# One scaling instruction for rows 0 to 3, the second tile's statistics in free order, tile 3's statistics on ScalarE, and a newly searched order

## The chip, the cores and the metric

The kernel runs on one core of one Trainium2 chip. The metric is the device time of one execution in microseconds (us); several executions are timed and their median is given. Engines are named as in the profile: PE (TensorE matmul), PEld (its weight loads), DVE (VectorE), ACT (ScalarE), POOL (GpSimd), SP (SyncE, which here only starts DMAs).

## The reference

The input x has 2048 rows of 640 bf16 values. It is normalized row by row, and then two branches and x itself are added.

```python
xn = _layernorm(x, axis=-1)            # (x - mean) / sqrt(var + 1e-5)
# branch A: spectral filter over rows and columns
X = rfft2(xn.astype(float32)); X = X * (w_r + 1j * w_i); a = irfft2(X).astype(bfloat16)
# branch B: gated linear unit without an activation
g = xn @ w_gate; u = xn @ w_up; b = (g * u) @ w_down      # 640 -> 1536 -> 640
out = x + a + b
```

## The kernel before

The 2048 rows are held as 16 tiles of 128 rows (128 partitions, 640 values each). Everything is one program of some 980 tasks. A task is a name, an engine, a function that emits its instructions, the buffers that it reads and writes, and, for a PE task, the PSUM bank (of eight) that it fills and the task that empties it.

The order is not decided while the program is built. The tuple `_PLAN` lists every task by number with its engine (0 PE, 1 ACT, 2 DVE, 3 POOL, 4 SP) and its PSUM bank. `replay` walks through it, gives every engine its queue in that order, and `compute_waits` puts a semaphore wait ahead of a task for each input, each output buffer and each PSUM bank that is not yet known to be free. Each task carries a duration in ns; in this file it only serves `replay`'s own clock, by which `compute_waits` sorts tasks when it leaves out waits that another wait already covers. The plan itself was found by a search that used such durations. [...]

The tasks that this study speaks of, in the order of the data:

- `ld_x0` to `ld_x5` (L728) load x: tiles 0, 1, 2 and 3 each alone, then four tiles, then eight. `ld_gw*` load gate and up weights.
- `warm_zero` (L696) clears a small tile on DVE; `warm` (L720) is 40 matmuls of that tile, which nobody reads; `fill` (L709) is 10 smaller ones. They keep PE occupied ahead of the first tile.
- Statistics of a tile b: on DVE `bn_b_0`, `bn_b_1` (written bn0_0 and so on, L756, one half of the columns each) and `ag` (L765); or on ACT `sm` (L738, the mean through an accumulator) and `sq` (L747, the sum of squares). Before, tiles 0 to 5 use DVE and tiles 6 to 15 use ACT. `sd` (L774, L775) is the square root on ACT and `rs` (L782) the reciprocal on DVE.
- Scaling: for tiles 0 to 3 `sub` (L792) subtracts the mean and `mul` (L798) multiplies; for tiles 4 to 15 one `mul` (L799) does both.
- Transposing: tiles 0 to 3 on PE (`T0_b`, L818) with copies out of PSUM by ACT and DVE (`eT0_b`), later tiles by DMA (`xt`).
- Branch B: `GU_f_b` multiplies weights of column block f with the rows that start at tile b (L968 for 128 or 256 rows, L948 for 512); `eG_u_0` and `eG_u_1` copy the two results of unit u from PSUM to a ring of three slots, and `H_u` (L984, L985) multiplies them on DVE. So a GU of unit u waits for H of unit u - 3. `ACC_a_h_k` (L1224) are the products with w_down, in pieces, and `FINA`, `FIN` and `st_out` finish and store.
- Branch A: `S1` to `S5` (DVE, five groups of tiles, L860 to L895), `R` (PE, L908) and `eR` (copy), then for t = 0 to 15 `D_t_w` (PE, L1025), `eD_t_w` (two copies of 64x321), `C_t` (L1045), `WM_t` (six DVE instructions from PSUM, L1062 and L1068), `NS_t` (three POOL instructions, L1077 to L1079), and for odd t `SM_t` (L1089, L1090), `JA_t` and `JB_t` (ACT or DVE). `IA_q` (L1116, L1118) with its copy `eIA_q`; when all of these are there, `I_a` (L1147), its copy `eI_a`, `V1` to `V5` (DVE), and `IV_a_h` (L1236), which adds the result to the bank that ACC fills.

Copies that either engine may do go through one helper: on ACT they are recorded at L684, on DVE at L685.

The lines that tie the second to the fourth tile to the tile ahead, and those that choose the statistics' engine:

```python
aset = set(opts.get("act_set", ())) | set(range(opts.get("act_stats", 6), 16))
...
if 1 <= b <= 3:
    bns[0].deps.add(muls[b - 1])
```

The first half of the statistics of tiles 1, 2 and 3 thus waits for the scaling of the tile ahead.

Of the kernel before, what the change touches and what calls it, by code (L numbers as in the profile page):

```python
# [399 lines left out]
def _d_act(n):  # L400
# [4 lines left out]
    (12, 4, -1), (0, 1, -1), (13, 4, -1), (176, 1, -1), (175, 4, -1), (8, 2, -1), (19, 2, -1), (9, 3, -1), (177, 4, -1),  # L405
    (18, 2, -1), (20, 2, -1), (11, 0, 0), (23, 2, -1), (21, 1, -1), (22, 2, -1), (24, 2, -1), (29, 2, -1), (25, 0, 2),
    (28, 2, -1), (26, 1, -1), (27, 2, -1), (178, 4, -1), (10, 0, 4), (14, 4, -1), (30, 2, -1), (33, 2, -1), (31, 1, -1),
    (32, 2, -1), (187, 0, 5), (34, 2, -1), (185, 0, 4), (188, 1, -1), (35, 0, 6), (15, 4, -1), (37, 2, -1), (192, 0, 5),
    (190, 0, 0), (186, 1, -1), (189, 2, -1), (38, 2, -1), (179, 4, -1), (36, 1, -1), (39, 2, -1), (180, 4, -1), (181, 4, -1),
    (197, 0, 1), (40, 2, -1), (48, 2, -1), (41, 1, -1), (43, 2, -1), (42, 2, -1), (193, 1, -1), (195, 0, 2), (44, 2, -1),  # L410
    (47, 2, -1), (202, 0, 3), (200, 0, 4), (182, 4, -1), (191, 1, -1), (196, 1, -1), (198, 1, -1), (49, 2, -1), (50, 1, -1),
    (16, 4, -1), (194, 2, -1), (201, 1, -1), (45, 0, 2), (52, 2, -1), (51, 2, -1), (183, 4, -1), (53, 2, -1), (207, 0, 6),
    (46, 1, -1), (184, 4, -1), (199, 2, -1), (118, 2, -1), (54, 0, 7), (205, 0, 2), (1, 4, -1), (203, 1, -1), (204, 2, -1),
    (55, 1, -1), (210, 0, 3), (212, 0, 7), (217, 0, 5), (208, 1, -1), (17, 4, -1), (215, 0, 4), (119, 2, -1), (206, 1, -1),
    (209, 2, -1), (120, 2, -1), (56, 2, -1), (211, 1, -1), (60, 2, -1), (59, 2, -1), (2, 4, -1), (3, 4, -1), (57, 2, -1),
    (68, 1, -1), (69, 1, -1), (213, 1, -1), (220, 0, 0), (121, 2, -1), (4, 4, -1), (58, 2, -1), (70, 1, -1), (216, 1, -1),
    (61, 2, -1), (218, 1, -1), (62, 1, -1), (122, 2, -1), (63, 2, -1), (222, 0, 1), (5, 4, -1), (214, 2, -1), (64, 2, -1),
    (125, 0, 2), (221, 1, -1), (71, 1, -1), (223, 1, -1), (123, 0, 6), (126, 1, -1), (219, 2, -1), (227, 0, 4), (127, 2, -1),
    (232, 0, 5), (225, 0, 0), (72, 1, -1), (230, 0, 1), (224, 2, -1), (128, 2, -1), (6, 4, -1), (7, 4, -1), (228, 1, -1),
    (66, 2, -1), (78, 1, -1), (79, 1, -1), (237, 0, 4), (226, 1, -1), (129, 2, -1), (235, 0, 0), (73, 2, -1), (80, 1, -1),  # L420
    (233, 1, -1), (229, 2, -1), (81, 1, -1), (130, 2, -1), (231, 1, -1), (82, 1, -1), (240, 0, 5), (76, 2, -1), (131, 2, -1),
    (238, 1, -1), (134, 0, 2), (74, 2, -1), (236, 1, -1), (83, 2, -1), (234, 2, -1), (242, 0, 4), (84, 2, -1), (65, 4, -1),
    (245, 0, 1), (67, 4, -1), (241, 1, -1), (75, 4, -1), (88, 1, -1), (77, 4, -1), (239, 2, -1), (135, 1, -1), (252, 0, 0),
    (247, 0, 5), (136, 2, -1), (243, 1, -1), (89, 1, -1), (244, 2, -1), (246, 1, -1), (132, 0, 2), (137, 2, -1), (90, 1, -1),
    (91, 1, -1), (86, 2, -1), (248, 1, -1), (250, 0, 1), (249, 2, -1), (255, 0, 4), (92, 1, -1), (98, 1, -1), (251, 1, -1),
    (85, 4, -1), (87, 4, -1), (437, 4, -1), (438, 4, -1), (93, 2, -1), (99, 1, -1), (138, 2, -1), (439, 4, -1), (253, 1, -1),
    (257, 0, 5), (256, 1, -1), (100, 1, -1), (258, 1, -1), (96, 2, -1), (254, 2, -1), (101, 1, -1), (139, 2, -1), (260, 0, 1),
    (262, 0, 0), (267, 0, 4), (94, 2, -1), (263, 1, -1), (133, 1, -1), (102, 1, -1), (261, 1, -1), (259, 2, -1), (140, 2, -1),
    (265, 0, 5), (103, 2, -1), (266, 1, -1), (440, 4, -1), (268, 1, -1), (270, 0, 0), (143, 0, 2), (264, 2, -1), (441, 4, -1),
    (104, 2, -1), (272, 0, 1), (124, 1, -1), (141, 0, 4), (269, 2, -1), (442, 4, -1), (108, 1, -1), (271, 1, -1), (273, 1, -1),  # L430
    (277, 0, 6), (149, 2, -1), (274, 2, -1), (109, 1, -1), (275, 0, 7), (280, 0, 0), (443, 4, -1), (142, 1, -1), (282, 0, 1),
    (444, 4, -1), (276, 1, -1), (278, 1, -1), (147, 0, 4), (281, 1, -1), (445, 4, -1), (145, 0, 6), (150, 2, -1), (446, 4, -1),
    (285, 0, 0), (106, 2, -1), (110, 1, -1), (283, 1, -1), (447, 4, -1), (146, 1, -1), (111, 1, -1), (287, 0, 1), (279, 2, -1),
    (112, 1, -1), (144, 1, -1), (292, 0, 6), (151, 2, -1), (286, 1, -1), (290, 0, 7), (293, 1, -1), (113, 2, -1), (448, 4, -1),
    (284, 2, -1), (152, 2, -1), (288, 1, -1), (116, 2, -1), (291, 1, -1), (297, 0, 2), (474, 4, -1), (475, 4, -1), (289, 2, -1),
    (476, 4, -1), (295, 0, 3), (114, 2, -1), (153, 2, -1), (302, 0, 0), (294, 2, -1), (162, 2, -1), (298, 1, -1), (296, 1, -1),
    (95, 4, -1), (97, 4, -1), (105, 4, -1), (299, 2, -1), (303, 1, -1), (154, 0, 6), (148, 1, -1), (107, 4, -1), (300, 0, 1),
    (477, 4, -1), (301, 1, -1), (156, 0, 2), (158, 0, 4), (159, 1, -1), (305, 0, 0), (155, 1, -1), (478, 4, -1), (160, 0, 4),
    (310, 0, 1), (479, 4, -1), (163, 2, -1), (480, 4, -1), (481, 4, -1), (307, 0, 6), (308, 1, -1), (304, 2, -1), (115, 4, -1),
    (312, 0, 7), (306, 1, -1), (164, 2, -1), (315, 0, 6), (317, 0, 0), (309, 2, -1), (313, 1, -1), (157, 1, -1), (311, 1, -1),  # L440
    (165, 2, -1), (316, 1, -1), (320, 0, 1), (318, 1, -1), (166, 2, -1), (322, 0, 0), (173, 0, 2), (314, 2, -1), (161, 1, -1),
    (167, 0, 6), (323, 2, -1), (321, 1, -1), (169, 0, 4), (174, 2, -1), (168, 1, -1), (325, 0, 1), (171, 0, 6), (170, 1, -1),
    (172, 1, -1), (327, 0, 0), (326, 2, -1), (451, 0, 1), (319, 2, -1), (324, 2, -1), (456, 0, 2), (328, 1, -1), (117, 4, -1),
    (449, 0, 3), (452, 2, -1), (458, 0, 4), (330, 0, 5), (435, 4, -1), (482, 0, 6), (450, 1, -1), (457, 1, -1), (436, 4, -1),
    (459, 2, -1), (705, 4, -1), (507, 4, -1), (508, 4, -1), (453, 0, 0), (509, 4, -1), (337, 0, 7), (510, 4, -1), (329, 2, -1),
    (460, 0, 2), (491, 0, 4), (511, 4, -1), (483, 1, -1), (512, 4, -1), (332, 0, 6), (331, 1, -1), (492, 1, -1), (515, 0, 5),
    (338, 1, -1), (454, 2, -1), (333, 1, -1), (516, 1, -1), (461, 2, -1), (335, 0, 0), (484, 0, 1), (455, 3, -1), (513, 4, -1),
    (340, 0, 4), (514, 4, -1), (485, 1, -1), (463, 2, -1), (342, 0, 5), (486, 0, 6), (522, 0, 1), (334, 2, -1), (336, 1, -1),
    (465, 2, -1), (540, 4, -1), (464, 1, -1), (489, 0, 0), (347, 0, 2), (541, 4, -1), (466, 0, 3), (462, 3, -1), (343, 1, -1),
    (487, 2, -1), (490, 1, -1), (468, 0, 5), (517, 0, 0), (493, 0, 6), (467, 1, -1), (523, 1, -1), (339, 2, -1), (345, 0, 3),  # L450
    (494, 2, -1), (496, 2, -1), (488, 3, -1), (542, 4, -1), (543, 4, -1), (352, 0, 1), (544, 4, -1), (545, 4, -1), (518, 1, -1),
    (346, 1, -1), (546, 4, -1), (341, 1, -1), (470, 0, 0), (472, 0, 3), (547, 4, -1), (344, 2, -1), (573, 4, -1), (469, 1, -1),
    (350, 0, 6), (473, 1, -1), (497, 2, -1), (524, 0, 7), (548, 0, 3), (348, 1, -1), (519, 0, 4), (353, 1, -1), (351, 1, -1),
    (495, 3, -1), (525, 1, -1), (357, 0, 2), (498, 2, -1), (520, 2, -1), (505, 0, 1), (574, 4, -1), (355, 0, 6), (358, 1, -1),
    (471, 1, -1), (499, 0, 7), (501, 0, 2), (349, 2, -1), (500, 2, -1), (550, 0, 0), (506, 1, -1), (356, 1, -1), (503, 0, 1),
    (526, 0, 4), (360, 0, 6), (521, 3, -1), (354, 2, -1), (583, 0, 7), (575, 4, -1), (549, 1, -1), (551, 1, -1), (576, 4, -1),
    (577, 4, -1), (362, 0, 3), (527, 2, -1), (578, 4, -1), (529, 2, -1), (530, 2, -1), (361, 1, -1), (555, 0, 0), (367, 0, 6),
    (579, 4, -1), (502, 1, -1), (365, 0, 2), (580, 4, -1), (359, 2, -1), (552, 0, 4), (363, 1, -1), (364, 2, -1), (528, 3, -1),
# [64 lines left out]
def _build(nc, A_x, A_w_r, A_w_i, B_w_gate, B_w_up, B_w_down, out, opts=None):  # L523
    opts = opts or {}
    tabs = _build_tables()
    es = contextlib.ExitStack()
    with es:
# [33 lines left out]
        b_sm = alloc("SM", 384)  # L561
        b_gbf = alloc("GBF", 6 * 512)
        b_stat = alloc("STAT", 608)
        b_dum = alloc("DUM", 256)
        b_jk = alloc("JK", 640)

        o_3 = cur[0]
# [780 lines left out]
```

## Time and profile before

| what | value |
|---|---|
| time, median of 3 | 199.64 us (199.36 to 199.67) |
| the profiled execution | 199.54 us, span of the program's instructions 197.2 us |
| granted PE clock | full over the span by the page's row |
| ACT ACTIVATE PSUM to SBUF, 128x512 f32 to bf16 | 87 of them, mean 599 ns |
| ACT copies of 64x321 (eD) | 60 of them, mean 434 ns |
| DVE BATCH_NORM_STATS2, 128x320 (bn) | 12 of them, mean 478 ns |
| DVE TENSOR_SCALAR 128x640: L792 / L798 / L799 | mean 380 / 386 / 441 ns |
| ACT statistics 128x640: L738 / L747 | mean 740 / 836 ns, with an accumulator read of 201 / 204 ns after each |

"Busy" in the page is the time in which an instruction of that engine stands in the trace. Matmuls overlap in it, so the share of PE tells that PE always has something under way, and the distance from one start to the next tells what a matmul takes. Times in a timeline count from the start of the span. A line such as "L684 ACT" is the helper's, so a copy is recognised by its shape or its place in the queue. Names of tasks were put to the instructions of the trace by their order on each engine, which is the plan's. A task's time is given as the start of its first and the end of its last instruction.

### The profile page before, as it was taken

What the parts mean: (1) busy time and instruction counts of PE and PEld (TensorE: products, weight loads), DVE (VectorE), ACT (ScalarE), POOL (GpSimd) and SP (SyncE); (2) the same over time, 40 slices, a digit from 0 to 9 for tenths busy, and PEclk for the clock granted to TensorE, in tenths of its full rate; (3) what the DMA queues carried; (4) which work ended last, traced back from release to release, by engine and by line L of the source; (5) the groups of instructions that cost most, each with busy time, mean ns of one, the idle gap of its engine ahead of it and who ended that gap; (6) DMA issues with size and microseconds to landing.
All of it is one profiled execution on the core that took longest, in us unless ns stands there. A gap on an engine that the chain in (4) does not pass through costs nothing.

```text
span 197.2 us, 4300 instructions
## 1 busy us (share of the span) xinstructions
PE 192.8 (98%) x1623; PEld 123.5 (63%) x1623; DVE 177.8 (90%) x396; ACT 138.0 (70%) x299; POOL 28.4 (14%) x53
## 2 busy tenths in 40 slices
PE   7999999999999999999999999999999999999995
PEld 7898645444555555555555555457777777777774
DVE  3799999999999989999898998995999999989753
ACT  3378999999965789999999999966414342335220
POOL 0000000000000003544163460760000000000000
PEclk9999999999999999999999999999999999999999
DMA  6999995245548232532552402003400434233412
GB/s 182 307 328 372 389 128 100 47 118 115 130 94 286 97 82 53 134 100 56 120 145 58 119 17 66 2 3 111 122 3 0 136 100 124 75 103 117 149 70 67
DMA packets 29667, 23.78 MB, mean 121 GB/s; under 512 B 10576, under 2 KB 27600, under 8 KB 29520
## 3 DMA queue, kind: packets, MB, share of 16 engines
q1 hardware_dynamic: 28848, 23.16, 42.3%
q10 hardware_dynamic: 800, 0.36, 0.6%
q8 instruction: 13, 0.21, 0.5%
q14 instruction: 6, 0.05, 0.1%
HBM read 18.92 MB, written 2.62 MB: 109 GB/s over the span
## 4 chain that ended last, share of the span: by engine, by line
PE 72%; ACT 13%; DVE 5%; SPq 4%; DMA 4%; issue 1%
PE ps L948 33%; PE ps L1224 26%; ACT arena L684 7%; SPq L678 4%; DMA arena<-in_A_x_dram 4%; ACT arena L747 3%; ACT arena L738 3%; PE ps L1147 2%; PE ps L1236 2%; PE ps L1116 2%; PE ps L1025 2%; PE ps L1045 2%; PE ps L908 2%; DVE arena L1062 1%; DVE arena L685 1%; PE ps L1118 1%
## 5 line engine op out<-in xcount | busy, mean ns | idle before, releaser
L684 ACT ACTIVATE arena<-ps 128x512 bf16<-128x512 f32 (+6 forms) x245 | 118.5, 525 | 49.5 <-PE ps L1236 21.1
L948 PE MATMUL ps<-arena 128*128 128x512 bf16 x420 | 97.5, 379 | 0.3 <-ACT arena L684 0.2
L948 PEld LDWEIGHTS ps<-arena 128*128 128x128 bf16 x420 | 38.7, 98 | 41.6 <-ACT arena L684 1.4
L1224 PE MATMUL ps<-arena 128*128 128x320 bf16 (+2 forms) x396 | 57.2, 295 | 0.0
L1224 PEld LDWEIGHTS ps<-arena 128*128 128x128 bf16 x396 | 37.5, 98 | 13.3
L1077 POOL COPY arena<-arena 128x126 bf16<-128x126 bf16 x16 | 9.3, 582 | 104.4 <-DVE arena L1068 104.4
L1062 DVE TENSOR_TENSOR arena<-ps,arena 128x256 bf16<-128x256 f32 x64 | 22.6, 416 | 1.5 <-PE ps L1045 1.0
L984 DVE TENSOR_TENSOR arena<-arena 128x512 bf16<-128x512 bf16 x42 | 17.8, 424 | 0.7
L968 PE MATMUL ps<-arena 128*128 128x128 bf16 (+1 forms) x160 | 13.9, 246 | 0.4 <-issue 0.3
L968 PEld LDWEIGHTS ps<-arena 128*128 128x128 bf16 x160 | 12.3, 98 | 1.6 <-issue 0.7
L1079 POOL TENSOR_SCALAR arena<-arena 128x130 bf16<-128x130 bf16 x16 | 11.7, 728 | 0.0
L1263 DVE TENSOR_TENSOR arena<-arena 128x640 bf16<-128x640 bf16 x15 | 7.2, 486 | 4.3 <-ACT arena L684 4.1
L685 DVE CAST arena<-ps 128x512 bf16<-128x512 f32 (+3 forms) x15 | 8.4, 578 | 2.4 <-PE ps L1118 1.7
L1025 PEld LDWEIGHTS ps<-arena 128*128 128x128 bf16 x160 | 7.5, 98 | 3.9 <-ACT arena L684 0.7
L1116 PEld LDWEIGHTS ps<-arena 128*128 128x128 bf16 x128 | 7.8, 119 | 3.1 <-issue 0.8
L1025 PE MATMUL ps<-arena 128*128 128x64 bf16 (+1 forms) x160 | 8.7, 193 | 0.3 <-ACT arena L684 0.3
L1078 POOL COPY arena<-arena 128x126 bf16<-128x126 bf16 x16 | 8.6, 538 | 0.0
L1116 PE MATMUL ps<-arena 128*128 128x64 bf16 x128 | 8.4, 199 | 0.1
L747 ACT ACTIVATE arena<-arena 128x640 bf16<-128x640 bf16 x10 | 8.4, 836 | 0.1
L1068 DVE TENSOR_TENSOR arena<-ps,arena 128x130 bf16<-128x130 f32 x32 | 8.0, 293 | 0.0
L860 DVE TENSOR_TENSOR arena<-arena 128x768 f32<-128x768 bf16 (+1 forms) x10 | 7.9, 792 | 0.0
L1236 PE MATMUL ps<-arena 128*128 128x320 bf16 (+2 forms) x33 | 7.6, 295 | 0.0
(65 smaller groups left out, 204.6 us busy)
## 6 DMA issues: line engine op xcount, KB each, us to landing
arena<-in_A_x_dram SPq DMA_DIRECT2D x20, 160.0 KB, 2.8
arena<-in_A_w_r_dram SPq DMA_DIRECT2D x30, 80.2 KB, 2.2
arena<-in_A_w_i_dram SPq DMA_DIRECT2D x30, 80.2 KB, 2.2
out_dram<-arena SPq DMA_DIRECT2D x15, 160.0 KB, 1.8
arena<-in_B_w_gate_dram SPq DMA_DIRECT2D x4, 320.0 KB, 5.5
arena<-in_A_x_dram SPq DMA_DIRECT2D x1, 1280.0 KB, 10.0
arena<-c_tf SPq DMA_DIRECT2D x4, 256.0 KB, 10.2
arena<-c_ti SPq DMA_DIRECT2D x2, 512.0 KB, 5.4
```

Source lines behind the costliest of these rows:

```text
L684: return c.e.activation(dst, src, _ACTF.Copy)
L685: return c.e.tensor_copy(dst, src)
L747: return c.e.activation(v_jk, v_x[:, b, :], _ACTF.Square, scale=-1.0, bias=v_m32[:, b:b + 1], accum_out=v_ss[:, b:b + 1])
L948: ins = c.e.matmul(ps[:, bk, :], v_gw[:, w, j, ft, :], v_xt[:, j, rows], start=(j == 0), stop=(j == 4))
L968: ins = c.e.matmul(ps[:, bk, w * n:(w + 1) * n], v_gw[:, w, j, ft, :], v_xt[:, j, rows], start=(j == 0), stop=(j == 4))
L984: return c.e.tensor_tensor(v_ht[:, ft0, rows], v_gbf[:, rr, 0, :], v_gbf[:, rr, 1, :], _OP.mult)
L1025: ins = c.e.matmul(ps[:, bk, k * 64:k * 64 + n], v_uq[:, k, t, :], v_fd[:, k * 128 + w * n: k * 128 + w * n + n], start=True, stop=True)
L1062: c.e.tensor_tensor(dst, xh, wv, _OP.mult)
L1079: return c.e.tensor_scalar(yg[:, :, 128:193], yg[:, :, 256:321], -1.0, None, _OP.mult)
L1116: c.e.matmul(ps[:, bk, 64 * k:64 * k + 64], yl[:, k:512:4], v_ti[:, q, 0, :], start=True, stop=True)
L1224: ins = c.e.matmul(ps[:, bk, 0:sl3.stop - sl3.start], v_ht[:, ft, a * 128:(a + 1) * 128], v_wd[:, ft, sl3], start=(ft == _FT_ORDER[0]), st ...
L1236: return c.e.matmul(ps[:, bank_of(own), 0:sl3.stop - sl3.start], v_sm[:, 2, :], v_v[:, a, sl3], start=False, stop=True)
```

## The change

There are five edits to tasks and one to the order.

1. The warm-up and filler matmuls read a constant tile of ones that the program has anyway (set by POOL ahead of the kernel's first instruction). `warm_zero` is gone. There are 12 fillers instead of 10.
2. `act_set` is `(3,)`: the statistics of tile 3 are `sm3` and `sq3` on ACT, instead of `bn3_0`, `bn3_1` and `ag3` on DVE.
3. The two lines that made the first half of a tile's statistics wait for the scaling of the tile ahead are gone.
4. `sub_apart` is 0: tiles 0 to 3 are scaled by one instruction with two operations, as the later ones are. `sub0` to `sub3` are gone.
5. Durations in the planner are other ones: eD 1040 on DVE and 899 or 1030 on ACT (910 and 880 before), NS 2000 (1180), SM 1540 (1420), JA and JB 1200 on ACT (985 by the formula before), and small ones.
6. `_PLAN` is a new one.

```diff
-        def em_wz(c):
-            return c.e.memset(v_dum, 0.0)
-        T("warm_zero", "dve", 150.0, em_wz, writes=[(b_dum, None)], prio=-1.0)
...
-        nfill = opts.get("nfill", 10)
+        nfill = opts.get("nfill", 12)
...
-                ins = c.e.matmul(ps[:, bk + (i % 2), (i % 4) * 128:(i % 4 + 1) * 128], v_dum[:, 0:128],
-                                 v_dum[:, 128:256], start=True, stop=True)
+                ins = c.e.matmul(ps[:, bk + (i % 2), (i % 4) * 128:(i % 4 + 1) * 128], v_one, v_one, start=True, stop=True)
...
-        aset = set(opts.get("act_set", ())) | set(range(opts.get("act_stats", 6), 16))
+        aset = set(opts.get("act_set", (3,))) | set(range(opts.get("act_stats", 6), 16))
...
-                    if 1 <= b <= 3:
-                        bns[0].deps.add(muls[b - 1])
...
-                if b < opts.get("sub_apart", 4):
+                if b < opts.get("sub_apart", 0):
                     def em_sub(c, b=b, mean=mean):
...
-                ed = T("eD_%d_%d" % (t, w), ("act", "dve"), {"dve": 910.0, "act": 880.0},
+                ed = T("eD_%d_%d" % (t, w), ("act", "dve"), {"dve": 1040.0, "act": (899.0, 1030.0)[w]},
...
-            T("NS_%d" % t, "pool", 1180.0, em_ns,
+            T("NS_%d" % t, "pool", 2000.0, em_ns,
```

The plan's numbers tell a reader nothing, so here are the queues that they stand for, where the study speaks of them.

```
DVE before: warm_zero bn0_1 bn0_0 ag0 sub0 rs_0 mul0 bn1_1 bn1_0 eT0_0 ag1 sub1 rs_1 mul1 eT0_1 H_0 bn2_0 bn2_1
            ag2 bn3_1 sub2 rs_2 mul2 bn3_0 ag3 H_1 sub3 rs_3 mul3 H_2 S1_0 ...
DVE after:  bn0_1 bn0_0 bn1_0 ag0 bn1_1 rs_0 ag1 mul0 rs_1 mul1 eT0_0 eT0_1 bn2_0 bn2_1
            ag2 H_0 eG_1_1 rs_2 eG_1_0 mul2 H_1 rs_3 mul3 H_2 S1_0 ...
ACT before: sd_0 eT0_0 sd_1 eG_0_1 eG_0_0 eT0_1 sd_2 eG_1_1 eG_1_0 eG_2_0 eG_2_1 sd_3 eG_3_0 eT0_2 eG_3_1 eT0_3 ...
ACT after:  sd_0 sd_1 eT0_0 eT0_1 eG_0_1 eG_0_0 sm3 sd_2 sq3 sd_3 eG_2_0 eG_2_1 eT0_2 eG_3_0 eG_3_1 eT0_3 ...
PE before:  warm T0_0 fill GU_1_0 GU_0_0 T0_1 GU_3_0 GU_2_0 GU_1_1 GU_0_1 GU_3_1 GU_2_1 T0_2 GU_5_0 T0_3 GU_4_0 GU_0_2 ...
PE after:   warm T0_0 fill T0_1 GU_1_0 GU_0_0 GU_0_1 GU_3_0 GU_2_0 GU_1_1 GU_3_1 GU_2_1 T0_2 GU_4_0 T0_3 GU_5_0 GU_0_2 ...

DVE before (around H_13): S3_2 mul11 H_13 S4_2 mul10 H_14     after: S3_2 rs_7 H_13 S4_2 H_14 S5_2 mul11
ACT before (around JA_1): eD_2_1 eG_30_0 JA_1 eG_31_1 eD_3_0  after: eD_3_1 eG_30_0 eD_3_0 eG_30_1 JA_1 eG_31_1
POOL before: NS_0 ... NS_5 NS_7 NS_6 ... NS_11 NS_13 NS_12 NS_14 NS_15    after: NS_0 to NS_15 in order
```

SP's queue is the same in both, to the last DMA. Tasks that change between ACT and DVE: eG_27_1, eR_15, eIA_4, eIA_11, JB_7, eG_41_1, eIA_16, eG_49_1, eIA_31, eI_0 and eI_13 go from DVE to ACT; eG_1_1, eG_1_0, eR_12, eG_35_0, eD_9_1, eIA_13, eIA_14, JA_9, JA_11, eIA_30, eG_49_0 and eI_2 go from ACT to DVE. On PE the same products are done in another order throughout.

## The prediction

> **What bounds the kernel now.** I read the page's busy shares first, then the timeline of the first 24 us, then the chain that ended last, and last the busy times of one stretch in the middle. The shares:
>
> ```profile
> PE 192.8 (98%) x1623; PEld 123.5 (63%) x1623; DVE 177.8 (90%) x396; ACT 138.0 (70%) x299; POOL 28.4 (14%) x53
> ```
>
> PE is always busy, with DVE close behind. A matmul of 512 columns starts every 216 ns (five in 1.08 us in the chain below). I took such a pitch for each width (320: 136 ns, 256: 109, 128: 56, 64: 29) and subtracted it from the distances between the starts of PE's matmul records. Streaming takes 187.8 of the 194.8 us to the last matmul's end; 1.0 lies before the first, 6.0 is the rest. Of that, 1.95 is the warm-up at half clock and about 1.0 the wait for the first tile, up to the first product at 6.77. So a new order can win back the time to 6.77 and about 2.4 us of later stalls; the rest is fixed work. The start:
>
> ```profile
> 1.04 4.45 PE L720 MATMUL ps<-arena 128*128 128x128 bf16 x40 [1.04 <-DVE arena L696]
> ...
> 4.34 0.29 ACT L775 ACTIVATE arena<-arena 128x1 f32<-128x1 f32 x1 [1.32 <-DVE arena L765]
> 4.35 0.39 DVE L792 TENSOR_SCALAR arena<-arena 128x640 bf16<-128x640 bf16 x1
> ...
> 4.87 0.39 DVE L798 TENSOR_SCALAR arena<-arena 128x640 bf16<-128x640 bf16 x1
> ...
> 5.40 0.69 PE L818 MATMUL ps<-arena 128*128 128x128 bf16 x5
> ...
> 6.77 1.34 PE L968 MATMUL ps<-arena 128*128 128x128 bf16 x20
> ...
> 8.67 3.51 PE L968 MATMUL ps<-arena 128*128 128x128 bf16 x60 [0.28 <-issue]
> ```
>
> See that the subtraction (L792) runs while ACT takes the square root (L775): it costs the first tile little. PE stands still before 8.67, where the landing records have the second pair of weight tiles at 8.57. The later stalls, in the chain (start, length, what):
>
> ```profile
> 39.55 0.50 ACT arena L684
> 40.17 3.40 PE ps L948 x15
> ...
> 79.91 1.86 ACT arena L684 x3
> 81.78 0.45 ACT arena L684
> 82.28 0.32 PE ps L1025 x5
> ...
> 128.65 0.45 ACT arena L684
> 129.14 2.33 PE ps L948 x10
> ```
>
> PE stands still 0.39 us before 40.17 (GU_2_4_1 waits for H_13, which ends on DVE at 40.02), 0.45 before 82.28 (for ACT's eD_3_0), 0.14 at 107.10, 0.29 at 128.26 (IA_24 waits for POOL's NS_12, which ends at 128.11, since the order puts NS_13 first), 0.22 at 129.14 and 0.19 before I_1 at 135.66. From I_1 on there is none. In the stretch from the first eD on DVE to the end of JB_15:
>
> ```profile
> 71.93:133.28 61.35, 60.88 (x569) 33.79 (x566) 57.66 (x153) 57.72 (x127) 28.00 (x48) 1.00 0.29 76
> ```
>
> the columns after the length are busy us of PE, PEld, DVE, ACT and POOL. Three engines are nearly full: whoever is late holds the others. Of DVE's 3.7 us idle, 2.33 are ten waits of 0.10 to 0.68 (the longest at 119.77, 103.92 and 82.91); the rest are steps of 0.03 between dependent operations.
>
> [...] 107 ns between 128-column matmuls up to 6.94, 56 after. [...]
>
> **The change part by part.**
>
> *Warm-up from a constant.* Without the memset at 0.81 to 0.98 the 40 matmuls start near 0.75, where the other engines' first instructions stand, and end near 5.0. Nothing waits for them: 0. The bound above is the clock, below.
>
> *First two tiles.* In DVE's new order bn1_0 stands before ag0. Tile 1 landed at 4.04, so bn1_0 runs 4.06 to 4.54, ag0 4.47 to 4.67 (before: 4.10), the root on ACT 4.71 to 5.00, bn1_1 beside it; rs_0 5.04, ag1 5.12, mul0 5.25. One fused instruction (L799, 441 ns) replaces two (380 and 386), so mul0 ends at 5.69 and T0_0 starts at 5.83 (before 5.40; 0.14 after mul0 in both). Worse by 0.43. rs_1 and mul1 follow, 5.68 to 6.32. PE: T0_0, 12 fillers, T0_1; from 6.94 at full clock the first product starts near 7.2 (before 6.77). But T0_1 (0.28) is now ahead of it, and GU_3_0, now fourth, comes at 8.9, past the landing at 8.57: the 0.44 stall is gone. So -0.28 - 0.44 + 0.45 is about -0.27 before GU_3_1. That one waits for H_0, which DVE runs after tile 2's statistics (tile 2 landed at 9.03: bn2 9.05, ag2 9.97, H_0 10.10 to 10.38), so 10.55 at best.
>
> *Tiles 2 and 3.* sm3 waits for tile 3 (9.52) and sd_2 is queued behind it on ACT: sm3 9.54 to 10.28, sd_2 ends near 10.70, 0.19 later than before, then rs_2 and eG_1_0, mul2 to 11.59. eG_1_1 and eG_1_0 are now on DVE; 256 columns from PSUM aren't in the trace; from 487 (320) and 688 (512), 1.05 ns a column, I take 420. T0_2 starts at 11.73 (before 12.01), GU_4_0 at 12.01. sq3 ends 11.40, sd_3 11.82, mul3 12.49: T0_3 fits behind GU_4_0. Then GU_5_0, and GU_0_2 at 14.50 against 14.85: -0.35. Best -0.45, because R_1 six units on needs a table that landed at 20.85; worst +1.2, the clock rival.
>
> *DVE up to S5_4.* Out: bn3_1 0.35, bn3_0 0.53, ag3 0.13, sub2 0.29, sub3 0.30 (start to next start), 1.60 together. In: two eG 0.68, H_0 0.20, fusing 0.06. So S5_4 ends 0.66 sooner, 67.55. H_13 no longer stands behind mul11 (0.35), so the 0.39 stall at 40.17 should go: PE reaches R_15, which waits for S5_4, at 68.30 - 0.35 - 0.39 = 67.56. Both agree: the D stage starts 0.65 sooner. If ACT, full from 16.89 to 40.05, holds PE at 40, it starts as before (third rival).
>
> *From D to I.* DVE gives ACT eIA_4, eIA_11, eIA_16, JB_7 and eG_41_1 (2.52) and takes eG_35_0, eD_9_1, eIA_13, eIA_14, JA_9 and JA_11 (3.44): +0.92. ACT by rows: out 599 + 868 + 2 x 438 + 2 x 1051, in 3 x 438 + 1051 + 599: 1.5 us less. eD_3_0 now precedes JA_1 and ends near 79.1 instead of 82.22, which removes DVE's 0.36 at 82.91 and PE's 0.45; NS_12 precedes NS_13, which removes 0.29. Not each of the ten waits can be followed: none to all of 2.33 comes back, I take half, 1.15. Net -0.23, bounds +0.92 and -1.41.
>
> *Longer durations in the code* only set the planner's wait bookkeeping: 0. SP's order is the same to the last DMA; POOL's differs in two exchanged pairs of NS. From I on the same matmuls are permuted; 24 ACC pieces stand before IV_0_1 in both, and V5_0 keeps its slack of 0.2: 0, bound +0.3 where slacks of 0.15 to 0.2 exist at 150.
>
> Sum: -0.65 - 0.23 = -0.88, on the profiled span 197.2 to 196.3. That run took 199.54, and the three shown 199.36 to 199.67, so the constant 2.3 around the span carries over: 199.64 - 0.88 = 198.76.
>
> **Rivals.** *All waits come back* (for it: ACT is relieved by 1.5 where it was full): -0.65 - 1.41 = -2.06, 197.6. *DVE's added 0.92 isn't absorbed* (for it: DVE 57.7 of 61.35): -0.65 + 0.92 = +0.27, 199.9. *ACT eats the start's gain*: -0.23, 199.4. *Slower: the clock.* The warm-up ends at 5.0 and PE idles until 5.83, where it idled 0.13 before. [...] GU_0_2 starts at 16.06, +1.2; 0.39 is absorbed at 40.17 and 0.23 in the middle: +0.6, 200.2. [...] *The change doesn't act* can be left out: the removed instructions are visible work.
>
> **How the numbers follow.** Main case 0.42 (own range 198.2 to 199.2), all waits 0.16, ACT 0.10, DVE 0.14, clock 0.18. A measurement tells 0.2%, 0.4 us, from no change. Faster: 0.40 + 0.16 + 0.04 + 0.02 + 0.02 = 0.64. Same: 0.02 + 0.06 + 0.05 + 0.03 = 0.16. Slower: 0.07 + 0.13 = 0.20. Leaving out the outer part of the best and of the clock case (0.07 each), the range is 197.7 to 200.4.
>
> **What would show it.** T0_0 near 5.8, the first product near 7.2, GU_0_2 near 14.5, no stall at 40, the first eD on DVE near 71.3, less than 1.3 us of idle beyond the 0.03 steps on DVE until JB_15, and I starting near 134.8. It is wrong if 128-column matmuls run at 107 ns after 7 us, if GU_0_2 isn't before 14.85, or if DVE's waits from D to I don't shrink.

## The result, and the profile after

| kernel | median us (range, executions) | before on the same chip | ratio, 95% interval |
|---|---|---|---|
| changed, first comparison | 198.42 (198.30 to 198.76, 4) | 199.64 | 0.9945 [0.9928, 0.9962] |
| changed, second comparison | 198.97 (198.33 to 199.73, 19) | 199.65 | 0.9966 [0.9954, 0.9977] |

The changed kernel is faster: by 1.22 us in the first comparison (0.88 was forecast), by 0.68 in the second. Its executions spread over 1.4 us, more than the difference of the two. The profiled execution of the first comparison took 198.3 with a span of 196.4, where the kernel before had 197.2. The page's shares:

```profile
PE 190.5 (97%) x1609; PEld 123.0 (63%) x1625; DVE 175.7 (89%) x390; ACT 138.6 (71%) x301; POOL 26.5 (14%) x53
```

PE's 1,609 matmuls stand beside 1,625 weight loads: 16 matmul records are missing, so the smaller busy time is no less work. DVE lost 2.1 us and ACT gained 0.6. The timeline of the start (start, length, engine, line, what; in brackets the idle time before):

```profile
0.76 3.90 PE L715 MATMUL ps<-const-bfloat16-1.0 128*128 128x128 bf16 x40 [0.76 <-PEq L1325]
...
5.34 0.45 DVE L791 TENSOR_SCALAR arena<-arena 128x640 bf16<-128x640 bf16 x1
...
5.93 0.44 PE L810 MATMUL ps<-arena 128*128 128x128 bf16 x5 [1.28 <-DVE arena L774]
```

The one scaling instruction of the first tile (L791, 0.45) ends at 5.78 and T0_0 starts at 5.93, 0.53 later than before. But PE's 40 warm-up matmuls needed 3.90 us instead of 4.45: the clock records show full clock from 3.89 here, from 6.94 before. (The page's clock row is full in every slice of both kernels, so it hides the slow start; the distances between the starts of the warm-up's matmuls show it: 107 ns from the second on up to 3.80 and 57 to 60 from 3.90 on here, 107 up to the last one before.) The same view of PE alone, a longer stretch:

```profile
7.04 4.68 PE L960 MATMUL ps<-arena 128*128 128x128 bf16 x80
11.57 0.44 PE L810 MATMUL ps<-arena 128*128 128x128 bf16 x5
```

All 80 matmuls of the first group run in one piece, without the stall before 8.67. T0_2 starts 0.45 sooner than before. The chain of waits (start, length, what):

```profile
39.60 0.60 DVE arena L881
40.54 0.60 DVE arena L886
...
79.31 0.60 ACT arena L683
79.93 1.06 ACT arena L683
...
82.22 1.03 PE ps L940 x4
```

The stall of 0.39 at 40 is gone: the chain runs through DVE there. At 80 a new one stands in the place of the old one: IA_0 waits 0.67 on PE, to 81.34, for JA_1 (the ACT piece at 79.93), the last of five in ACT's queue, which ACT works one after the other and without a gap from 77.01. At 128 one stand-still of 0.27 is left of two (0.29 and 0.22). The same stretch as before, from the first eD on DVE to the end of JB_15 (length, then busy us of PE, PEld, DVE, ACT, POOL):

```profile
71.31:132.78 61.47, 60.32 (x560) 34.25 (x567) 58.50 (x155) 57.10 (x126) 26.10 (x48) 1.00 0.29 76
```

It isn't shorter: 61.47 against 61.35, with 0.84 more work on DVE and 0.6 less on ACT. DVE's waits over 0.05 add up to 1.63, from 2.33.

Followed task by task, the lead over the kernel before is 0.53 us at GU_0_2 (14.32), 0.67 at the end of S5_4, 0.62 at the first D, 0.63 at the first eD on DVE, 0.50 at the end of JB_15, 0.80 at the first I matmul and at the last matmul, and 0.8 in the span. The other 0.4 of the 1.22 lies outside the span: time less span is 1.83 to 1.93 in every execution of the changed kernel and 2.15 to 2.5 in the kernel before.

### The profile page after: what moved, and what is told of

Its sections match the earlier page's. It is cut to its first block, busy times and chain, and to the rows that moved or that the text cites. A ratio compares the mean times of both kernels' runs of the same rounds, so it can differ in the third digit from the quotient of the medians.

```text
span 196.4 us, 4281 instructions
## 1 busy us (share of the span) xinstructions
PE 190.5 (97%) x1609; PEld 123.0 (63%) x1625; DVE 175.7 (89%) x390; ACT 138.6 (71%) x301; POOL 26.5 (14%) x53
## 4 chain that ended last, share of the span: by engine, by line
PE 68%; DVE 16%; ACT 6%; issue 4%; DMA 3%; SPq 2%
PE ps L940 29%; PE ps L1216 27%; ACT arena L683 5%; DMA arena<-in_A_x_dram 3%; PE ps L1108 2%; PE ps L1139 2%; PE ps L1228 2%; DVE arena L853 2%; DVE arena L791 2%; PE ps L1037 2%; DVE arena L976 2%; PE ps L1017 2%; DVE arena L852 2%; SPq L677 2%; DVE arena L864 1%
## 5 line engine op out<-in xcount | busy, mean ns | idle before, releaser
L940 PE MATMUL ps<-arena 128*128 128x512 bf16 x404 | 95.6, 379 | 0.9
L1216 PE MATMUL ps<-arena 128*128 128x320 bf16 (+2 forms) x396 | 57.4, 295 | 0.1
L1069 POOL COPY arena<-arena 128x126 bf16<-128x126 bf16 x16 | 7.6, 474 | 105.8 <-DVE arena L1060 105.8
L1071 POOL TENSOR_SCALAR arena<-arena 128x130 bf16<-128x130 bf16 x16 | 12.2, 760 | 0.0
L684 DVE CAST arena<-ps 64x321 bf16<-64x321 f32 (+4 forms) x17 | 9.1, 547 | 2.1 <-PE ps L1110 1.0
L741 ACT ACTIVATE arena<-arena 128x640 bf16<-128x640 bf16 x11 | 9.2, 833 | 0.1
L732 ACT ACTIVATE arena<-arena 128x640 bf16<-128x640 bf16 x11 | 8.1, 740 | 1.4 <-DMA arena<-in_A_x_dram 1.3
L750 DVE BATCH_NORM_STATS2 arena<-arena 128x6 f32<-128x320 bf16 x10 | 4.4, 479 | 5.0 <-DMA arena<-in_A_x_dram 4.9
```

Source lines behind the costliest of these rows:

```text
L684: return c.e.tensor_copy(dst, src)
L741: return c.e.activation(v_jk, v_x[:, b, :], _ACTF.Square, scale=-1.0, bias=v_m32[:, b:b + 1], accum_out=v_ss[:, b:b + 1])
L940: ins = c.e.matmul(ps[:, bk, :], v_gw[:, w, j, ft, :], v_xt[:, j, rows], start=(j == 0), stop=(j == 4))
L1071: return c.e.tensor_scalar(yg[:, :, 128:193], yg[:, :, 256:321], -1.0, None, _OP.mult)
L1216: ins = c.e.matmul(ps[:, bk, 0:sl3.stop - sl3.start], v_ht[:, ft, a * 128:(a + 1) * 128], v_wd[:, ft, sl3], start=(ft == _FT_ORDER[0]), st ...
```

## The experiments

After the first comparison two theories stood for the whole: A, the gain is made inside the span by the new order; B, part of it is made outside the span by the constant that took the memset's place. Later ones are named as they come. Each kernel was compared with the kernel before on its own chip, so across chips the ratios are compared, not the times.

| kernel | median us (range, executions) | before | ratio, 95% interval |
|---|---|---|---|
| w_const | 199.23 (199.03 to 199.66, 18) | 199.65 | 0.9978 [0.9971, 0.9985] |
| start_after | 199.79 (199.48 to 200.75, 14) | 199.65 | 1.001 [0.9999, 1.002] |
| start_before | 199.34 (198.84 to 199.96, 10) | 199.65 | 0.9981 [0.997, 0.9993] |
| warm_48 | 198.45 (198.35 to 198.53, 5) | 199.78 | 0.9934 [0.992, 0.9949] |
| after_memset | 198.72 (198.18 to 199.05, 6) | 199.78 | 0.9945 [0.9926, 0.9963] |
| ja1_early | 198.28 (198.12 to 198.31, 5) | 199.78 | 0.9925 [0.9911, 0.9939] |
| both | 198.33 (198.13 to 198.82, 6) | 199.78 | 0.993 [0.9915, 0.9945] |
| warm_24 | 200.28 (200.13 to 201.17, 6) | 199.56 | 1.0047 [1.0031, 1.0062] |
| ja_thin | 198.46 (198.39 to 198.82, 5) | 199.56 | 0.995 [0.9938, 0.9962] |
| tile3_dve | 200.19 (200.16 to 200.42, 5) | 199.56 | 1.0039 [1.0026, 1.0052] |
| sub_apart | 198.61 (198.32 to 198.71, 5) | 199.56 | 0.9952 [0.994, 0.9964] |

**The changed kernel again.** No edit.

> The changed kernel once more, as the measure for the three beside it. Time 0.9945 of before with an interval of about 0.002, span 0.8 us shorter than that of before. Theory A (all of the gain lies in the order of work inside the span): time minus span is the same in both kernels, so the 1.2 us against 0.8 us of the first comparison was scatter of single executions. Theory B (some 0.4 us lie outside the span): time minus span is 1.9 here and 2.3 in before, again.

The profiled execution took 199.63 with a span of 197.7, against 198.3 and 196.4. The timeline of PE alone:

```profile
6.05 0.69 PE L810 MATMUL ps<-arena 128*128 128x128 bf16 x5 [0.87 <-DVE arena L774]
...
7.71 5.68 PE L960 MATMUL ps<-arena 128*128 128x128 bf16 x80
```

T0_0 takes 0.69 instead of 0.44, as it did in the kernel before, and the same 80 matmuls take 5.68 instead of 4.68: PE is at half clock, and the clock records give full clock from 9.90. GU_0_2 comes at 15.97, 1.65 later than in the other execution, R_15 1.35 later, the span's end 1.3. The same program has both outcomes, and its 19 times go from 198.33 to 199.73. The expected span, 0.8 shorter than before, came in the first comparison's profile and not in this one; the median span of the 19 is 197.1, where the kernel before has 197.3. Time less span stayed at 1.83 to 1.93.

**Only the constant.** The kernel before with

```
-                ... v_dum[:, 0:128], v_dum[:, 128:256], start=True, stop=True)
+                ... v_one, v_one, start=True, stop=True)
-        nfill = opts.get("nfill", 10)
+        nfill = opts.get("nfill", 12)
```

and no memset; the order otherwise as before.

> The kernel before with the warm-up edit alone (constant of ones, no memset, 12 fillers), its order kept. Theory A: the clock is released near 3.9 us instead of 6.9, the first product comes earlier, but GU_3_0 still waits for weights that land at 8.57, so the span stays within 0.1 us of before. Rival 1: the earlier clock is what shortens the start, then GU_0_2 comes near 14.3 as in the changed kernel and the time falls by 0.5 us. Theory B: if the 0.4 us outside the span belong to the memset or its semaphore, time minus span falls to 1.9 here.

0.42 faster. The profiled span is 197.2, as before the change; time less span is 1.87 to 2.16. PE's timeline in the profiled execution, with full clock from 4.42:

```profile
6.57 1.28 PE L964 MATMUL ps<-arena 128*128 128x128 bf16 x20 [0.29 <-DVE arena L761]
7.68 0.44 PE L814 MATMUL ps<-arena 128*128 128x128 bf16 x5
8.74 1.44 PE L964 MATMUL ps<-arena 128*128 128x128 bf16 x23 [0.62 <-issue]
```

Even with the clock early, the old order then waits at 8.74 for the second pair of weight tiles, and GU_0_2 comes at 14.94. So inside the profiled span nothing was won. Over all executions the median of time less span is 2.06, where the kernel before has 2.32, so most of what was won lies outside. That spoke for B.

**The two orders joined.** The first has the changed kernel's instructions and its order up to GU_5_0, mul3 and eG_4, then the order before; the second the other way round.

> Tasks of the changed kernel, its order up to mul3, T0_3, GU_4_0, GU_5_0 and eG_4, then the order of before (banks renamed to fit). Theory A: the start is worth 0.53 us at GU_0_2 and DVE's smaller work carries it past 40 us; nothing is lost later, so 0.5 us faster than before in the span (0.9973). Rival: the order of the middle is needed to keep it, ACT holds PE at 40 us, and the gain there is under 0.2 us.

> Tasks of the kernel before (with subtraction apart, statistics of tile 3 on DVE), its order up to the same place, then the order of the changed kernel. Theory A: GU_0_2 starts at 14.85 as before; the stall of 0.39 at 40 us goes because H_13 no longer stands behind mul11, and the middle gives 0.1 to 0.2 more, less what DVE's 0.66 us of additional work takes at R_15: 0.2 to 0.4 us faster than before (0.9985). Rival: the middle's order alone is worth 0.8 us or more, then it equals the changed kernel.

Start_after had GU_0_2 at 14.69, 0.16 ahead. Its timeline of PE at 40 us, then of DVE at 21 us:

```profile
40.10 3.40 PE L940 MATMUL ps<-arena 128*128 128x512 bf16 x14 [0.31 <-DVE arena L976]
```

```profile
20.99 0.17 DVE L774 RECIPROCAL arena<-arena 128x2 f32<-128x2 f32 x1 [0.33 <-ACT arena L767]
```

PE waits at 40 for H_13 again, which comes only 0.07 sooner than before the change. DVE had lost its lead long before: it was 0.33 at H_2 (12.62) and 0.07 at 20.99, where rs_4, the reciprocal of tiles 4 and 5, waits for the square root (sd_4). ACT's old order starts it 3.84 after sm6, the new one 3.22 after. R_15 is 0.07 ahead, the last matmul 0.04. So the rival's size came true, and ACT is the cause, but at 21 us by way of DVE and not on PE at 40. Although start_after has the constant, its time less span is 2.3 to 2.6, so B in this form doesn't hold.

Start_before kept the memset and had 1.8 to 2.1. It lost 0.20 up to GU_0_2, 0.23 up to R_15, and then its first I came 0.05 later than before the change: between R_15 and I the new order is worth 0.18. Its profiled span is no shorter than that of the kernel before (197.3; 197.2). What it gained, 0.31, lies outside, so that its ratio is near the expected one is luck.

**A longer warm-up, the memset again, and JA_1.** For the spread of the changed kernel theory C was set up: the clock, with full clock from 3.89 in one of its profiles and from 9.90 in the other. That PE's stand-still ahead of T0_0 decides between the two was the author's estimate.

```
 warm_48       -nwarm = opts.get("nwarm", 10)     +nwarm = opts.get("nwarm", 12)
 after_memset  +T("warm_zero", "dve", 150.0, em_wz, writes=[(b_dum, None)], prio=-1.0)
 ja1_early     ACT: eD_3_0 -eG_30_1 JA_1   ->   eD_3_0 JA_1 eG_30_1
```

> The changed kernel with 48 warm-up matmuls in place of 40; all else as it is. Theory C (the clock): the changed kernel's times spread over 1.4 us (198.33 to 199.73) because PE stands still between the warm-up's end (near 5.0 at half clock) and T0_0 (5.93)[...]. With 48 matmuls at 107 ns the warm-up ends near 5.9[...]. Expected: times within 0.6 us of one another, median near 198.4, ratio 0.994. Rival D (the spread has another cause, such as the landings of the first tiles, or the part of the time outside the span): spread of 1.2 us or more, median 198.9 to 199.1, ratio 0.996 to 0.997. A third answer: the longer warm-up holds up T0_0 and costs its own 0.1 to 0.2 us with no change in the spread.

> The changed kernel with the warm-up and the fillers reading zeros again, that DVE writes first, as in the kernel before; all else as changed. Theory B (the constant saves 0.4 us outside the span: time less span 1.9 in the changed kernel, 2.3 to 2.4 before): time less span is 2.3 again, the median 0.4 above the changed kernel's 198.97, near 199.3. Rival (that difference goes with something else in the program, as start_after with 2.5 although it has the constant suggests): time less span 1.8 to 2.0, and the median is set by the clock alone: the warm-up starts 0.28 later and ends later, so the gap in front of T0_0 is 0.6 instead of 0.9 and the late clock is rarer: 198.5 to 198.9.

> The changed kernel with one instruction moved: JA_1 ahead of eG_30_1 on ACT. In the changed kernel's profile IA_0 waits 0.67 us on PE at 81.34 for JA_1, the last of five that stand in ACT's queue. Theory E (PE's waits between D and I are what is left to win there): JA_1 ends near 80.35, IA_0 starts at 80.7 without a stall, PE runs ahead 0.6 us, DVE's waits behind PE (WM_3 0.29, others) shrink, JB_15 and I come 0.4 to 0.6 us sooner: median 0.3 to 0.6 below the changed kernel's 198.97, 198.4 to 198.7. Rival F (DVE's work of 58.5 in 61.5 us sets the stretch, the stall on PE is absorbed by it anyway): JB_15 and I move by less than 0.15, median 198.8 to 199.1.

> The 48 warm-up matmuls and JA_1 ahead of eG_30_1 together. With theories C and E the gains add: median 198.4 less 0.3 to 0.5, 197.9 to 198.1, ratio 0.992. With C alone 198.4, with E alone 198.4 to 198.7 and a spread of 1.4; with neither 199.0.

Warm_48 came out as C says: five executions within 0.18, median 198.45. In its profile the 48 warm-up matmuls take 4.17 us, where 107 ns each would make 5.1, so full clock came during them. Five of ja1_early, with the short warm-up, spread no more (0.19), so the spread of five decides nothing. After_memset: time less span 1.74 to 2.11 and not the 2.3 of B, so B falls for good.

Ja1_early shows what the stall at 81 is worth. PE's timeline, then ACT's:

```profile
80.88 0.30 PE L1108 MATMUL ps<-arena 128*128 128x64 bf16 x4
...
81.69 0.45 PE L1037 MATMUL ps<-arena 128*128 128x321 bf16 x2 [0.25 <-ACT arena L683]
```

```profile
79.47 1.05 ACT L683 ACTIVATE arena<-arena 64x1024 bf16<-64x1024 bf16 x1
80.55 2.80 ACT L683 ACTIVATE arena<-ps 128x512 bf16<-128x512 f32 x6
```

JA_1 (the 64x1024 copy) ends at 80.52, and IA_0 starts at 80.88 almost without a wait. But C_3 (L1037) then stands still for 0.41 before 81.69: its banks of PSUM come free with eG_30_1 and eG_31_1, which JA_1 has pushed back on ACT; the second ends at 81.63. ACT has no gap from 77 to 83. Of 0.67 on PE, 0.18 is left as a gain between the first D and the first I (63.72 against 63.90). The size is nearer to rival F, the cause is neither: ACT's queue. The kernel named both had a further stall of 0.61 before GU_3_0 at 9.45, at a full clock from 4.17: PE waits there for a load of up weights. Tile 2 came late as well (its statistics start at 9.80, in warm_48 at 9.07). So the gains didn't add in that profile; the median of 198.33 is a miss for the sum of 198.0. It also shows that landings move between executions, as rival D had it: with 48 warm-up matmuls the six times of both still spread over 0.69. The clock is one cause of the spread, not shown to be the only one.

**Four that take away or give back one thing**, the last three with the 48 warm-up matmuls:

```
 warm_24    -nwarm = opts.get("nwarm", 10)                  +nwarm = opts.get("nwarm", 6)
 ja_thin    -def em_ja(c, lr=lr):                           +def em_ja(c, lr=lr, n=(1 if t in (9, 11) else None)):
 tile3_dve  -aset = set(opts.get("act_set", (3,))) | ...    +aset = set(opts.get("act_set", ())) | ...
 sub_apart  -if b < opts.get("sub_apart", 0):               +if b < opts.get("sub_apart", 4):
```

> The changed kernel with 24 warm-up matmuls in place of 40: the warm-up ends near 3.3 and PE stands still for 2.6 us in front of T0_0. Theory C (the clock): [...] GU_0_2 starts at 15.5 to 16.5 instead of 14.3. Median 199.4 to 200.0, above all but the slowest of the changed kernel's executions (198.33 to 199.73), ratio 0.998 to 1.001. Rival D (the spread of the changed kernel has another cause, and the warm-up's length is of no account): ratio as for the changed kernel, 0.9945 to 0.9966.

Full clock came at 8.99. PE's timeline:

```profile
0.76 2.72 PE L715 MATMUL ps<-const-bfloat16-1.0 128*128 128x128 bf16 x24 [0.76 <-PEq L1325]
5.97 0.69 PE L810 MATMUL ps<-arena 128*128 128x128 bf16 x5 [2.50 <-DVE arena L774]
```

T0_0 stood where it stands in the changed kernel (5.93) and ran at half clock (0.69 instead of 0.44); against warm_48, GU_0_2 came 1.15 later, at 15.49, and the last matmul 0.73 later. That is the price of the late clock after what is absorbed on the way. The span grew by 1.7, though. The rest is in the output's DMA issues (durations least, median, most; first and last start), first of warm_24, then of warm_48:

```profile
L677 SPq DMA_DIRECT2D out_dram<-arena x6: 332/387/1825, 188.1 to 196.2; - x6
```

```profile
L677 SPq DMA_DIRECT2D out_dram<-arena x6: 332/338/408, 187.4 to 194.6; - x6
```

One issue, at 193.87, took 1.83 us instead of 0.41, and the last two stood behind it on SP. The DMA view from 192 to 197 us has one packet of a queue that the profile calls "instruction" (packets, MB, share of 16 engines):

```profile
q8 instruction: 1, 0.02, 1.7%
```

By the DMA records it ran from 193.97 to 195.31, and the issue ended 0.38 after it. In the other thirteen profiles the last such packet starts between 188.4 and 190.9. After 30 us all profiles together have 20 SP issues of more than 1 us, DMA transposes left out. All 20 overlap such a packet, and 19 of them end 0.36 to 0.39 after it; 44 issues that overlap one are shorter than that. So the slow issue goes with the packet. That 32 fewer instructions on PE moved the packet to this place is a guess, not tested. All six executions have spans of 198.2 or more, so it isn't one execution's accident. Of the loss, 0.73 is the clock, about 0.9 isn't, and the ratio alone overstates C.

> The changed kernel with 48 warm-up matmuls, and with most of JA_9 and JA_11 on DVE left out: they copy one column in place of all of theirs, so a part of the operator's coefficients isn't formed. Takes about 0.75 us of work off DVE between D and I and puts it nowhere else. Theory F (DVE sets that stretch): JB_15, which ended at 132.78, and I_0 come 0.4 to 0.75 us sooner, ratio 0.990 to 0.9915 where the same kernel with JA_9 and JA_11 whole had 0.9934. Rival E (PE's stalls at 81, 128 and 135 set it, or ACT's queue): under 0.15 us, ratio 0.993 to 0.994.

DVE's timeline of ja_thin, then of warm_48:

```profile
118.63 0.17 DVE L684 COPY arena<-arena 64x4 bf16<-64x4 bf16 x1
...
122.05 1.42 DVE L1054 TENSOR_TENSOR arena<-ps,arena 128x256 bf16<-128x256 f32 x4 [0.57 <-PE ps L1037]
```

```profile
118.62 0.42 DVE L684 COPY arena<-arena 64x1024 bf16<-64x1024 bf16 x1
...
122.04 1.42 DVE L1054 TENSOR_TENSOR arena<-ps,arena 128x256 bf16<-128x256 f32 x4 [0.36 <-PE ps L1037]
```

The two copies gave back 0.25 each, less than the 0.75 together that the expectation took. All of it turned into waiting: WM_13 starts at 122.05 as ever, since C_13 on PE comes no sooner, and I_0 starts at 135.01 in both. Here F falls: DVE waits for PE in this part. (The ratios differ, 0.995 and 0.9934, on two chips and with intervals that overlap.)

> The changed kernel with 48 warm-up matmuls, and tile 3's statistics back on DVE (bn3_0, bn3_1 and ag3 behind mul2, about 1.0 us; sm3 and sq3 leave ACT; sd_3 behind eT0_2, T0_3 behind GU_5_0). Theory A (DVE runs without waits from 10 us to S5_4, which R_15 waits for): S5_4 and R_15 come 0.9 to 1.0 us later than in the changed kernel (67.5 and 67.7), the whole rest with them, ratio 0.998 to 0.9985 against 0.9934. Rival (slack takes it up: DVE's 0.3 us of small waits, or PE's stall at 81, which gets time to vanish): under 0.5 us at the end, ratio 0.9934 to 0.996.

PE's timeline, then DVE's:

```profile
12.72 2.34 PE L960 MATMUL ps<-arena 128*128 128x256 bf16 x20 [0.79 <-DVE arena L977]
14.90 0.44 PE L810 MATMUL ps<-arena 128*128 128x128 bf16 x5
16.14 1.05 PE L960 MATMUL ps<-arena 128*128 128x256 bf16 x8 [0.80 <-ACT arena L683]
```

```profile
11.29 0.88 DVE L750 BATCH_NORM_STATS2 arena<-arena 128x6 f32<-128x320 bf16 x2
12.21 0.21 DVE L757 BATCH_NORM_AGGREGATE arena<-arena 128x2 f32<-128x12 f32 x1
12.33 0.24 DVE L977 TENSOR_TENSOR arena<-arena 128x256 bf16<-128x256 bf16 x1
```

The statistics stand ahead of H_1 (L977), which GU_4_0 waits for, and ahead of mul3. PE stands still for about 0.95 twice; GU_0_2 is 1.80 late, R_15 and the end 1.43. More than the 0.9 to 1.0 of DVE work alone: in this place it costs PE too. A better place may exist and wasn't tried.

> The changed kernel with 48 warm-up matmuls, and rows 0 to 3 scaled in two instructions again (each subtraction directly ahead of its reciprocal, four in all). By the prediction's terms fusing saves DVE 0.59 less 0.06 for tiles 2 and 3, the first two standing ahead of the wait for tile 2's landing at 9.1: S5_4 and R_15 should come 0.5 to 0.7 us later than in the changed kernel, and T0_0 0.2 to 0.3 later, ratio 0.996 to 0.997 against 0.9934. Rival (the statistics on ACT alone carry the gain and the two shorter instructions hide under the wait for the square root): under 0.2 us, ratio 0.993 to 0.9945.

In DVE's timeline the subtraction and the scaling of the first tile:

```profile
5.23 0.37 DVE L784 TENSOR_SCALAR arena<-arena 128x640 bf16<-128x640 bf16 x1
5.52 0.16 DVE L774 RECIPROCAL arena<-arena 128x1 f32<-128x1 f32 x1
...
5.71 0.39 DVE L790 TENSOR_SCALAR arena<-arena 128x640 bf16<-128x640 bf16 x1
```

T0_0 is 0.36 late against warm_48, GU_0_2 0.34, S5_4 0.32 and what follows it 0.31: between the two expectations. Part of it isn't the edit's. Tile 1 landed later in this profile, so ag0 starts 0.23 later ahead of any subtraction (4.77; 4.54), and tile 2's statistics start 0.20 later (9.27; 9.07). DVE is 0.47 behind at H_2, so the two subtractions of tiles 2 and 3 cost it some 0.27 there. The later start of the first tile costs DVE nothing: it waits 1.47 us for tile 2 all the same.

## Why the prediction was right or wrong

The predicted 198.8 and a faster kernel were right, and so were most of its places: T0_0 (5.83; 5.93), the end of S5_4 (67.55; 67.54), the first eD (71.3; 71.31), the first I (134.8; 134.86). Step by step:

*Start, -0.35 at GU_0_2.* -0.53 with the clock early, +1.12 with it late. The order of the start did what was worked out; the clock, which the sum put at nothing, moves the same program by 1.65 us. T0_0 moves too, from 5.77 to 6.37 in the eleven profiles with the new start: with bn1_0 ahead of ag0 the first tile waits for the second one's landing (0.48 on DVE in start_after), which the sum took as fixed.

*The 40 us stall and DVE up to S5_4, -0.65 at the D stage.* Measured -0.62. That DVE's work sets this stretch holds from 20 us on: S5_4 ends 47.27 to 47.29 after the start of rs_4 in all eleven profiles that have the new order there, 47.14 or 47.15 in the three with the old one. Where rs_4 stands isn't a matter of DVE's sum alone, and this wait is missing in the prediction. Ja_thin's start was 0.20 earlier than that of warm_48; its timeline of ACT, then of DVE:

```profile
16.88 0.74 ACT L732 ACTIVATE arena<-arena 128x640 bf16<-128x640 bf16 x1 [0.85 <-DMA arena<-in_A_x_dram]
```

```profile
20.41 0.17 DVE L774 RECIPROCAL arena<-arena 128x2 f32<-128x2 f32 x1 [0.28 <-ACT arena L767]
```

ACT waits for the load of tiles 4 to 7, and DVE waits for ACT's square root; rs_4 starts at 20.41 as in warm_48, and S5_4 moves by nothing. In the changed kernel's first profile that load let ACT start at 16.71, 0.17 sooner, and the lead at S5_4 was 0.67; in warm_48 it is 0.52. So the agreement is in part luck. In start_after it is ACT's old order that holds rs_4. The rival "ACT eats the start's gain" is real there. The single terms were off: the subtractions of tiles 2 and 3 (0.59 less 0.06) cost some 0.27 at H_2 in sub_apart, and tile 3's statistics (1.01) cost 1.43 in the place tried. That H_13 behind mul11 made the wait at 40 wasn't tested alone.

*From D to I, -0.23.* From the first D to the first I it was 64.08 before and is 63.90 in the changed kernel: -0.18, and 63.88 to 63.91 in nine profiles with this order. The size was right, the reason failed. "Half of 2.33 back" was 0.70, not 1.15; DVE's "+0.92" was 0.84; together +0.14, and the stretch on DVE did grow, by 0.12. But I isn't set by DVE's sum: ja_thin took 0.5 off it and moved nothing. PE sets it, which stands still for only 1.34 us of this stretch before and 1.27 after, and at 81 ACT's queue behind PE (ja1_early). The stall at 81 wasn't foreseen. That the first I comes 0.30 sooner against JB_15 is the new order of PE's last pieces there; this is read from the order, not tested.

*After I, 0.* Measured 0: the lead is 0.80 at the first I and at the end.

*"The constant 2.3 around the span carries over."* This failed. It is 1.9 in the changed kernel, worth 0.4 us, about as much as the rest of the gain in the second comparison: there the medians less their usual rests (199.65 - 2.33 and 198.97 - 1.87) leave 0.2 inside the span. That the measured 0.68 is near the forecast 0.88 is then luck: the sum put 0.88 inside and nothing outside. The first comparison's profile, with its early clock, has the 0.80 inside.

*The clock rival.* A late full clock costs about what was forecast. Ten 128-column matmuls take 1.07 us until then and 0.56 after (107 and 56 ns from start to start in the kernel before). GU_0_2 at 16.06 was the author's estimate, and it came at 15.97; of 1.2, 0.6 was to be absorbed on the way, and it was 0.59 of 1.12 against the kernel before and 0.42 of 1.15 in warm_24. What failed is to take the time of full clock as a thing of the kernel. By the clock records it came at 3.44, 3.74, 3.80, 3.89, 3.96, 4.13, 4.17, 4.42, 4.43 and 6.94, at 8.99 in warm_24, and at both 3.89 and 9.90 in the changed kernel itself. So it is no case with a chance of its own but a spread within the changed kernel's executions. What sets this time the runs do not show. The total of that rival, 200.2, didn't come: the late execution's span was 0.5 longer than the one before the change, near the forecast 0.6, but it took 199.63, since 0.4 less lay outside the span.

What stays open is, first, what makes time less span 1.9 in one program and 2.3 in another. The constant and the memset are excluded (1.7 to 2.1 with the memset, 2.3 to 2.6 with the constant in start_after, 2.2 in tile3_dve). The DMA records give a clue: packets of 8 KB on another queue called "instruction" (q14) still run after the program's last instruction. In five profiled executions (before, w_const, start_after, start_before, after_memset) the last of them ends 2.10 to 2.85 after it, and time less span is this less 0.23 to 0.24. In eight it ends by 1.33 to 1.59, and time less span is 1.80 to 1.88. Tile3_dve (2.17; 2.19) fits neither. So the term goes with these packets in thirteen of fourteen; no run tests the cause. Open is, second, whether ja1_early and warm_48, whose ratios of 0.9925 and 0.9934 are the best seen, beat the changed kernel, which wasn't run on their chip.

## What to carry to other kernels

Where PE starts at half clock, one profile shows one time of full clock out of several (3.89 and 9.90 us in the same program, 1.65 us apart at GU_0_2): profile more than one execution before a gain at the start is counted, and try a longer warm-up as a run of its own. A stall removed on the fullest engine is worth only what the next engine in the chain leaves of it (0.67 became 0.18), so look up what stands ready behind it before it is counted. A gain at the start counts only up to the next wait for a load (rs_4 above). And compare spans as well as times: a difference outside the span is a term of the sum like any other.

## What was not expected of the hardware

Time less span differs by program (1.83 to 1.93, 2.15 to 2.5, 2.3 to 2.6) more than by execution, with the same first and last instructions in the profile, and goes with instruction packets that run on after the last instruction. A single DMA issue on SP took 1,825 ns where no output issue takes more than 410 in the other profiles, during a 16 KB instruction packet, and delayed the end by about 0.9 us.
